# A Fourier mixing layer with a gated feed-forward block: the first batch's stage of one kernel rearranged

## The chip, the cores and the metric

The kernel runs on one core of a Trainium2 chip. The core has a matrix engine (PE, with its weight loads shown as PEld), three engines for elementwise work (DVE, ACT, POOL), a sync engine (SP) that here only issues transfers, and 16 DMA engines that all queues share. Each engine works through its own instructions in the order written and waits on semaphores for the others. The metric is device time in microseconds (us), the median of several runs of the whole kernel.

## The reference

Input `x` is 8 batches of 3008 rows of 256 columns. Each batch gets a two-dimensional discrete Fourier transform, over the rows and over the columns, of which the real part is kept. The 24064 rows that result go through a gated feed-forward block with 1536 hidden columns.

```python
X = np.fft.fft(x, axis=1)
X = np.fft.fft(X, axis=2)
h = X.real                                  # 24064 x 256
g = h @ w_gate
out = (g / (1 + np.exp(-g)) * (h @ w_val)) @ w_out
```

## The kernel before

**The mathematics that the code uses.** The real part of the transform is a sum of cosine products less a sum of sine products. Row k and row 3008-k of a batch share both sums and differ in the sign of the second, so the kernel computes a tile `Pt` (cosine sums) and a tile `Qt` (sine sums) for half of the rows, 1504 per batch. The transform over the 256 columns is put into the weights once: `Wp` is the cosine table `CD` times the weights, `Wq` is the sine table `SDt` times the weights, for the gate and for the value matrix, and `Wm` is `Wq` scaled for the mirrored row.

**Folding.** The rows of a batch are split into four sets (`a` = 0 to 3) of 752. In each set a row that rises with the index is paired with one that falls, and in each pair column d is added to column 256-d, so that the sums run over a quarter of the data. The pairs 1 to 128 of each set form the long set, `XA`, and the last 60 the short set, which for the first batch is `XC0`: four slots of two halves of the partitions. The rises are in slots 0 to 3 of `XA` (0 and 1 of `XC0`), the falls in slots 4 to 7 (2 and 3).

**The first stage** computes the P and Q tiles 0 and 1, for the first batch, before the steady work can start. It is written out by hand, engine by engine (`tc.manual_schedule()`), and its steps are:

- The sync queue issues the loads: all of the long set's rises in one transfer of 1 MB, two falls, the short set's rises and falls. ACT's queue issues two falls (`fall_a`), POOL's queue one short load of middle rows and the weights (`load_w`), which it converts to bf16 on the way.
- PE runs 48 products of zeros (line 306), whose results nobody reads.
- The falls lie in another row order than the rises. A product with a 0/1 matrix (`place`, lines 433 to 442) turns the rises' rows over into the falls' order, in PSUM: `putA` for the long set, `putC` for the short one. These matrices are an iota compared with the partition's number.
- DVE adds rises and falls, the columns reversed (`cross`, or `cross_halves`, which does it in two halves), and adds or subtracts the halves (`half_fold`, line 460); `ends` does column 0. POOL does some of these folds (`fold_d`, line 497) and ACT casts the results to bf16 (`half_cast`).
- The cosine and sine tables `Tab` come from POOL (`turns`, line 364), DVE (`angles`, `magnitude`, lines 368 and 372) and ACT (`sine`, `cosine`).
- PE multiplies the folds with the tables into accumulators in PSUM: `acc[0]` are the even sums (P), `acc[1]` the odd ones (Q), each for the even columns' half q=0 and for q=1. `half_folded` adds the long set, `folded_c` the short set, `row0` some single rows.
- ACT copies `acc[eo][0]` (`even_copy`, line 517), and DVE adds it to and subtracts it from `acc[eo][1]` (`first_puts`, line 646), which gives the columns of `Pt` and `Qt`.
- `first_w` (line 505) multiplies the first 512 columns of the weights by `CD` and `SDt`, for the gate (`first_w(0, ...)`) and for the value matrix (`first_w(1, ...)`); the copies that it returns cast the products into `Wp` and `Wq`.
- `turn_signs` and `row_signs` compute a few signs per partition that later tables need.

**The steady work** goes over 24 tiles of 480 or 512 columns of P and Q and 12 blocks of 128 hidden columns: 288 units. In each PE forms the gate and the value for the rows and for the mirrored rows (`mm`, line 1015), ACT the SiLU, DVE and POOL the products, and one tile later PE multiplies by `w_out` (line 1279). In tile 0 every value product stays in its PSUM buffer, one of three, until DVE has multiplied it twice: `hp` (line 1053) for the rows, `hm` (line 1074) for the mirrored ones. The order of the steady work on every engine is computed when the kernel is built, by a planner with costs, windows and due times; it does not depend on when things happen on the chip. Between the units stand the remaining blocks of the weights (lines 1501 to 1516), and POOL's folds and the transforms of the next batches.

PSUM has eight banks of 512 float32 columns. Before, eight pools of one bank each serve both the first stage and the steady work: three `psG`, three `psV`, two `psO`.

## Time and profile before

| | us |
|---|---|
| median of 3 runs (lowest, highest) | 597.34 (597.27, 597.76) |
| profiled execution | 597.77 |
| its span, from the first to the last instruction | 596.0 |
| PE busy in the span | 590.9 |

The profile is one execution. A row of a timeline gives the start in us from the span's start, the duration, the engine, the line of the kernel, the operation, what it writes and reads with the shapes, and how many instructions the row merges; brackets tell how long the engine stood idle before it and who ended that. The ends of matmuls are modelled and overlap with the next one's start, so the distance between two starts is a better price of a matmul than its duration. DMA rows are packets, megabytes and the share of the time of 16 engines.

### The profile page before, as it was taken

How to read it: one execution, taken by the hardware profiler on the slowest of the kernel's cores; microseconds unless marked ns; L12 is line 12 of the kernel's file. 1: busy time of each engine (PE TensorE's matmuls, PEld its weight loads, DVE VectorE, ACT ScalarE, POOL GpSimd, SP SyncE). 2: the span in 40 equal slices, each digit the busy share in tenths (PEclk: the TensorE clock that was granted, in tenths of full speed). 3: DMA queues.
4: the chain of work that ended last, by engine and by line, in shares of the span. 5: the costliest groups of instructions: out<-in, count | busy, mean ns of one | idle time of the engine just before them, and what ended most of it. 6: DMA issues, size and time to landing. Idle time of an engine off the chain costs nothing.

```text
span 596.0 us, 12394 instructions
## 1 busy us (share of the span) xinstructions
PE 590.9 (99%) x4014; PEld 390.6 (66%) x4014; DVE 568.6 (95%) x1062; ACT 553.6 (93%) x1071; POOL 533.5 (90%) x491
## 2 busy tenths in 40 slices
PE   9999999999999999999999999999999999999997
PEld 6456676666666666666666666666666666666686
DVE  9989999999999999999999999999999999999993
ACT  8768989999998899899999999999999999999995
POOL 9979999999999999999899998999889868687782
PEclk9999999999999999999999999999999999999999
DMA  9976772756244255285125122054121103202212
GB/s 251 161 222 229 185 235 71 194 165 222 82 149 126 73 139 137 68 273 159 54 82 168 37 64 63 19 152 143 46 63 37 47 19 88 67 28 63 60 54 81
DMA packets 61070, 68.17 MB, mean 114 GB/s; under 512 B 6744, under 2 KB 48668, under 8 KB 61006
## 3 DMA queue, kind: packets, MB, share of 16 engines
q1 hardware_dynamic: 57422, 64.44, 36.1%
q0 software_dynamic: 3216, 2.36, 2.9%
q8 instruction: 31, 0.51, 0.4%
q10 hardware_dynamic: 368, 0.59, 0.3%
q14 instruction: 33, 0.27, 0.2%
HBM read 40.21 MB, written 35.43 MB: 127 GB/s over the span
## 4 chain that ended last, share of the span: by engine, by line
PE 96%; DVE 0%; ACT 0%; issue 0%
PE o L1279 41%; PE g L1015 27%; PE v L1015 21%; PE g L1453 2%; PE o L1453 2%; PE v L1279 1%; PE o L1501 1%; PE g L622 0%; PE o L622 0%; PE g L1279 0%; PE o L1582 0%; PE g L1650 0%; DVE Wp L508 0%; ACT es L1289 0%; DVE Qt L646 0%
## 5 line engine op out<-in xcount | busy, mean ns | idle before, releaser
L1226 POOL TENSOR_TENSOR hm<-sv 128x1024 bf16<-128x1024 f32 (+2 forms) x137 | 254.7, 1862 | 32.3 <-ACT sv L1202 12.9
L1218 DVE SCALAR_TENSOR_TENSOR sv<-es,v 128x512 f32<-128x512 f32 (+2 forms) x262 | 174.0, 670 | 5.9 <-PE v L1015 4.3
L1279 PE MATMUL o<-Wo,hm 128*128 128x256 bf16 (+1 forms) x1128 | 163.7, 273 | 0.0
L1279 PE MATMUL o<-Wo,hp 128*128 128x256 bf16 (+1 forms) x1104 | 161.1, 272 | 0.0
L1229 DVE TENSOR_TENSOR hp<-sp,v 128x512 bf16<-128x512 f32 (+2 forms) x228 | 151.6, 671 | 1.9 <-PE v L1015 1.1
L1279 PEld LDWEIGHTS <-hm 128*128 128x128 bf16 (+2 forms) x1140 | 111.9, 98 | 58.0 <-issue 0.6
L1279 PEld LDWEIGHTS <-hp 128*128 128x128 bf16 (+2 forms) x1140 | 111.8, 98 | 55.3 <-issue 0.3
L1202 ACT ACTIVATE sv<-g 128x512 f32<-128x512 f32 (+2 forms) x181 | 119.0, 675 | 3.6 <-PE g L1015 3.1
L1127 ACT ACTIVATE sp<-g 128x512 f32<-128x512 f32 (+2 forms) x181 | 112.1, 621 | 5.9 <-PE g L1015 4.0
L1015 PE MATMUL g<-Pt,Wp 128*128 128x512 bf16 (+2 forms) x288 | 107.5, 374 | 0.0
L1015 PE MATMUL v<-Pt,Wp 128*128 128x512 bf16 (+2 forms) x288 | 106.2, 375 | 0.2 <-DVE Wp L508 0.2
L1015 PE MATMUL g<-Qt,Wq 128*128 128x512 bf16 (+2 forms) x288 | 105.4, 375 | 0.1
L1088 ACT ACTIVATE v<-bc,w 128x512 f32<-128x512 bf16 (+2 forms) x139 | 100.3, 726 | 1.9 <-DVE sv L1218 1.0
L1152 DVE SCALAR_TENSOR_TENSOR es<-bc,w,v 128x512 f32<-128x512 bf16 (+2 forms) x135 | 97.9, 732 | 2.1
L1150 ACT ACTIVATE es<-v 128x512 f32<-128x512 f32 (+2 forms) x139 | 86.0, 621 | 3.2 <-PE v L1015 1.6
L1015 PEld LDWEIGHTS <-Wp 128*128 128x128 bf16 x576 | 56.3, 98 | 26.0 <-DVE Wp L508 1.0
L1015 PE MATMUL g<-Qt,Wm 128*128 128x512 bf16 (+2 forms) x195 | 73.1, 376 | 0.0
L1131 DVE SCALAR_TENSOR_TENSOR sg<-bc,w,g 128x512 f32<-128x512 bf16 (+2 forms) x93 | 67.3, 724 | 1.6 <-PE g L1015 1.4
L1235 POOL TENSOR_TENSOR hp<-sp,pp 128x512 bf16<-128x512 f32 (+1 forms) x46 | 57.2, 1245 | 8.0 <-ACT pp L1232 7.8
L1202 ACT ACTIVATE sv<-sg 128x512 f32<-128x512 f32 (+2 forms) x93 | 63.6, 695 | 0.5 <-DVE sg L1195 0.5
L1195 DVE SCALAR_TENSOR_TENSOR sg<-sg,g 128x512 f32<-128x512 f32 (+2 forms) x93 | 61.6, 663 | 0.2
L1015 PEld LDWEIGHTS <-Wq 128*128 128x128 bf16 x437 | 42.7, 98 | 27.5 <-issue 0.4
(218 smaller groups left out, 788.7 us busy)
## 6 DMA issues: line engine op xcount, KB each, us to landing
out_dram<-ev SPq DMA_DIRECT2D x96, 128.0 KB
XA<-in_x_dram SPq DMA_DIRECT2D x30, 256.0 KB
tA<-in_x_dram SPq DMA_DIRECT2D x28, 256.0 KB
XA<-tA SPq DMA_DIRECT2D x14, 512.0 KB
XC<-in_x_dram SPq DMA_DIRECT2D x28, 120.0 KB
tC<-in_x_dram SPq DMA_DIRECT2D x28, 120.0 KB
XC<-tC SPq DMA_DIRECT2D x6, 480.0 KB
bc<-br SPq DMA_DIRECT2D x19, 128.0 KB
```

The costliest lines, as they stand in the source:

```text
L1015: nc.tensor.matmul(ps[:, :n], Wt[:, gv, fs], src[:, :n], start=start, stop=stop, skip_group_check=True)
L1088: nc.scalar.activation(T_[kv][:, :w], bc[t][:, :w], AF.Copy, scale=w0[:, 1, f:f + 1])
L1127: nc.scalar.activation(sp_to()[:, :w], T_[kg][:, :w], AF.Silu)
L1131: nc.vector.scalar_tensor_tensor(T_[keg][:, :w], bc[t][:, :w], w0[:, 0, f:f + 1], T_[kg][:, :w], op0=Alu.mult, op1=Alu.add)
L1150: nc.scalar.activation(T_[kes][:, :w], T_[kv][:, :w], AF.Copy, scale=2.0 if on_pool(u) > 1 else 1.0)
L1152: nc.vector.scalar_tensor_tensor(T_[kes][:, :w], bc[t][:, :w], w0[:, 1, f:f + 1], T_[kv][:, :w], op0=Alu.mult, op1=Alu.add)
L1195: nc.vector.scalar_tensor_tensor(T_[kgm][:, :w], T_[keg][:, :w], 2.0, T_[kg][:, :w], op0=Alu.mult, op1=Alu.subtract)
L1202: nc.scalar.activation(sv()[:, f % 2, w - 1::-1, 1], T_[kgm if by_dve else kg][:, :w], AF.Silu)
L1218: nc.vector.scalar_tensor_tensor(sv()[:, f % 2, w - 1::-1, 0], T_[kes][:, :w], 2.0, T_[kv][:, :w], op0=Alu.mult, op1=Alu.subtract)
L1226: nc.gpsimd.tensor_tensor(hts_(t)[1][:, f - 1:f + 1, :w], sv()[:, :, :w, 1], sv()[:, :, :w, 0], op=Alu.mult)
L1229: nc.vector.tensor_tensor(hts_(t)[0][:, f, :wp], T_[ksp][:, :wp], T_[kv][:, :wp], op=Alu.mult)
L1279: nc.tensor.matmul(st["ps"][:n, j, :], hts[t][minus][:, f, c:c + n], Wo[:, f, :], start=(f == 0), stop=(f == nF - 1))
```

## The change

It touches the first stage only. The steady work has the same instructions in the same order on every engine.

- The long set's rises are loaded by two transfers, sets 0 and 1 and sets 2 and 3, with the falls between them; one of the falls changes queue.
- The middle rows of the short set are loaded by the sync queue, between its first two falls, and no longer by POOL.
- `putA` is filled and compared on POOL, between the two `turns`, and no longer on DVE.
- There are 33 products of zeros at the start and 6 after the placements, instead of 48 and 8.
- PSUM is laid out by six pools of its own while the first stage runs, two of them of two banks; the pools of the steady work are made after it. Sets 2 and 3 of the long set share a tile of two banks, and so do the two sets of the short set; `cross_halves` (long set), `half_fold` and `ends` take both at once. The short set is still crossed one set at a time.
- On PE both pairs of `first_w` come earlier: those of the gate ahead of the short set's even sums, those of the value matrix ahead of all odd sums. The odd sums and `row0` go first through q=0, then through q=1, and ACT's copy of q=0 stands between.
- On DVE `turn_signs` goes behind all `first_puts`, and the cast of the first value weights ahead of the second ones.
- On POOL the sums `EOb` of the odd half go ahead of the next weights' load, and `row_signs` and a memset go behind the first stage's other work. On ACT `weigh_ce` goes behind the casts, and the clearing of `Z0` behind `opposite(1)`.

```diff
+    first_ctx = ExitStack()
+    banks = [first_ctx.enter_context(tc.tile_pool(name=f"bank{i}", bufs=1, space=bass.MemoryType.PSUM)) for i in range(6)]
+    def two_banks(i):
+        return banks[i].tile([P, 2, T], F32, name=f"b{i}")
+    def one_bank(i):
+        return banks[i].tile([P, T], F32, name=f"b{i}")
...
-    q.dma_start(out=XA3[:, 0:4, :], in_=up_block(0, 1, P))
+    def rises_a(a):
+        q.dma_start(out=XA3[:, a:a + 2, :], in_=rows_at(0, R * a + 1, [[2 * D, P], [R * D, 2], [1, 2 * D]]))
...
+    rises_a(0)
     nc.scalar.activation(w0[:, 0, 0:1], zero, AF.Silu)
     fall_a(3, nc.scalar)
-    fall_a(2, q)
-    fall_a(1, nc.scalar)
+    rises_a(2)
+    fall_a(2, nc.scalar)
+    fall_a(1, q)
     fall_a(0, q)
     rises_c(q)
...
-    for a in range(2):
-        fall_c(1, a, q)
-        fall_c(0, a, q)
+    fall_c(1, 0, q)
+    q.dma_start(out=XC0[NCR:64 + NCR + 1:64, 2:4, 0], in_=rows_at(0, 0, [[2 * R * D, 2], [R * D, 2], [1, D]]))
+    fall_c(0, 0, q)
+    for hi in (1, 0):
+        fall_c(hi, 1, q)
...
+    warm(33)
...
-    vts(putA, putA, scalar1=pcol, scalar2=None, op0=Alu.is_equal)
...
     turns(ti[0], kf, 0)
+    nc.gpsimd.iota(putA, pattern=[[-LA, NA], [1, LA]], base=JA - 1, **iota)
+    pts(putA, putA, scalar1=pcol, scalar2=1.0, op0=Alu.is_equal, op1=Alu.mult)
     turns(ti[1], kf, 1)
     more_iotas()
-    nc.gpsimd.dma_start(out=XC0[NCR:64 + NCR + 1:64, 2:4, 0],
-                        in_=rows_at(0, 0, [[2 * R * D, 2], [R * D, 2], [1, D]]))
...
+    b0, b1, b23, bC = one_bank(1), one_bank(4), two_banks(0), two_banks(5)
+    ps0, ps1, ps23, psC = (of_sets(b) for b in (b0, b1, b23, bC))
+    for a, to in enumerate((b0, b1, b23[:, 0], b23[:, 1])):
+        place(to, XA, putA, a)
+    idle = bC
+    warm(6)
...
-    for a in range(2, 4):
-        cross_halves(FA[:, a, :, 1:P + 1], XA, psA, a)
-    for a in range(2, 4):
-        half_fold(0, EOA[0][1][:, a - 2], FA[:, a, :, 1:P + 1], psA, a)
-    for a in range(2, 4):
-        ends(Eh[:, a], XA, psA, a)
+    cross_halves(FA[:, 2:4, :, 1:P + 1], ps23, down23)
+    half_fold(0, EOA[0][1], FA[:, 2:4, :, 1:P + 1], ps23)
+    ends(Eh[:, 2:4], ps23, down23)
...
-    cross_halves(FC[:, 0], XC0, psC, 0)
-    half_fold(0, EB[:, 0, 0], FC[:, 0], psC, 0)
+    for a in range(2):
+        cross_halves(FC[:, a], psC[:, a], downC[:, a])
+    half_fold(0, EB[:, 0], FC, psC)
+    half_fold(1, EB[:, 1], FC, psC)
+    ends(Ec0, psC, downC)
+    first_ws = two_banks(0)
+    copies = [first_w(0, k, 1, first_ws[:, k]) for k in range(2)]
     folded_c(0, 0)
-    copies = [first_w(0, k, 1, p_.tile([P, T], F32, name=n_)) for k, (p_, n_) in enumerate(((psG, "g"), (psV, "v")))]
-    cross_halves(FC[:, 1], XC0, psC, 1)
-    half_fold(0, EB[:, 0, 1], FC[:, 1], psC, 1)
     folded_c(0, 1)
     od0 = even_copy(0)
+    second_ws = two_banks(5)
+    copies += [first_w(1, k, k, second_ws[:, k]) for k in range(2)]
+    start_acc(1, 1, 4)
...
     first_puts(0, od0, (0, 1))
+    for c in copies:
+        c()
     for i in range(2):
+        half_folded(1, 0, False, (i,))
         row0(0, i, acc[1][i])
-    copies[0]()
-    copies[1]()
-    turn_signs()
-    od1 = even_copy(1)
-    copies += [first_w(1, k, k, psO.tile([P, T], F32, name="o")) for k in range(2)]
-    first_puts(1, od1, (0,))
-    for c in copies[2:4]:
-        c()
-    first_puts(1, od1, (1,))
+        if i == 0:
+            od1 = even_copy(1)
+    first_puts(1, od1, (0, 1))
+    turn_signs()
     tmp_ctx.close()
+    first_ctx.close()
+
+    psG = Slots("psG", 3, space=bass.MemoryType.PSUM)
+    psV = Slots("psV", 3, space=bass.MemoryType.PSUM)
+    psO = Slots("psO", 2, space=bass.MemoryType.PSUM)
```

103 lines of the change are left out of this document (41 added, 62 removed).

## The prediction

> **What bounds the kernel.** I read the page's busy shares and chain first, then the timeline of each engine over the first 36 us.
>
> ```profile
> span 596.0 us, 12394 instructions
> PE 590.9 (99%) x4014; PEld 390.6 (66%) x4014; DVE 568.6 (95%) x1062; ACT 553.6 (93%) x1071; POOL 533.5 (90%) x491
> ...
> PE 96%; DVE 0%; ACT 0%; issue 0%
> ```
>
> PE carries the chain. The timeline of PE (start, duration, engine, line, operation, count, idle time before it in brackets) shows where it is not yet PE that decides:
>
> ```profile
> 1.04 5.30 PE L306 MATMUL o<-sel 128*128 128x128 bf16 x48 [1.04 <-DVE sel L258]
> 6.13 0.94 PE L438 MATMUL g<-XA,putA 128*128 128x512 f32 x1
> 7.33 1.02 PE L438 MATMUL v<-XA,putA 128*128 128x512 f32 x2
> ...
> 10.36 1.08 PE L438 MATMUL o<-XC,putC 128*128 128x512 f32 x2
> ...
> 14.00 0.59 PE L505 MATMUL g<-W,CD 128*128 128x512 bf16 x2
> 14.87 0.32 PE L493 MATMUL v<-Tab,EOf 128*128 128x378 bf16 x1
> ...
> 18.20 0.57 PE L1015 MATMUL g<-Pt,Wp 128*128 128x480 bf16 x2
> 18.90 0.36 PE L1015 MATMUL g<-Qt,Wq 128*128 128x480 bf16 x1
> 19.50 0.38 PE L1015 MATMUL v<-Pt,Wp 128*128 128x480 bf16 x1 [0.24 <-DVE Wp L508]
> ...
> 29.76 0.37 PE L1015 MATMUL v<-Pt,Wp 128*128 128x480 bf16 x1
> ```
>
> The steady work begins at 18.20, pauses until 18.90 for the first Q tile and until 19.50 for the cast of the first value weights; after that PE has no idle time worth a row. The first stage is worth what it moves the products at 18.90 and 19.50, if the engines that feed the next 16 us keep up. DVE runs it nearly without a pause:
>
> ```profile
> 3.50 0.61 DVE L355 TENSOR_SCALAR putA<-putA,pcol 128x128 f32<-128x128 f32 x1
> 4.02 1.36 DVE L368 SCALAR_TENSOR_TENSOR rr<-kf,mM,t 128x377 f32<-128x377 f32 x2
> ...
> 7.84 0.68 DVE L447 TENSOR_TENSOR FA<-g,XA 128x510 f32<-128x510 f32 x1
> ...
> 8.44 0.68 DVE L447 TENSOR_TENSOR FA<-v,XA 128x510 f32<-128x510 f32 x1
> ...
> 9.25 0.43 DVE L451 TENSOR_TENSOR FA<-g,XA 128x256 f32<-128x256 f32 x1
> ...
> 10.91 0.41 DVE L460 TENSOR_TENSOR XA<-FA,g 128x256 f32<-128x256 f32 x1
> ...
> 11.71 0.41 DVE L451 TENSOR_TENSOR FC<-o,XC 128x256 f32<-128x256 f32 x1
> ...
> 12.62 0.42 DVE L460 TENSOR_TENSOR EOf<-FC,o 128x256 bf16<-128x256 f32 x1
> ...
> 15.73 1.20 DVE L646 TENSOR_TENSOR Pt<-g,od 128x188 bf16<-128x188 f32 x5 [0.64 <-ACT od L517]
> ...
> 16.92 0.47 DVE L345 TENSOR_SCALAR n__445<-mm 128x4 int32<-128x4 f32 x1
> ...
> 18.07 0.77 DVE L646 TENSOR_TENSOR Qt<-g,od 128x188 bf16<-128x188 f32 x3
> ...
> 20.17 1.40 DVE L1053 TENSOR_TENSOR hp<-sg,v 128x480 bf16<-128x480 f32 x2 [0.25 <-ACT sg L1050]
> ...
> 28.94 0.64 DVE L1074 TENSOR_TENSOR hm<-sg,v 128x480 bf16<-128x480 f32 x1
> ```
>
> The timelines of POOL and ACT, and the sync queue's issues:
>
> ```profile
> 1.45 0.39 POOL L286 IOTA putA<- 128x128 f32 x1
> 2.13 2.86 POOL L364 TENSOR_SCALAR t<-kf,mM 128x377 int32<-128x377 f32 x4
> 6.45 0.84 POOL L406 TENSOR_SCALAR putC<-putC,pcol 128x128 f32<-128x128 f32 x1
> 8.32 0.82 POOL L394 DMA_DIRECT2D W<-in_moe_w_gate_dram  x1
> 18.89 1.35 POOL L512 TENSOR_SCALAR Wm<-Wq,m 128x512 bf16<-128x512 bf16 x2
> ...
> 15.23 0.47 ACT L517 COPY od<-v 128x377 f32<-128x377 f32 x1 [0.78 <-PE v L493]
> 17.10 0.47 ACT L517 COPY od<-v 128x377 f32<-128x377 f32 x1 [0.42 <-PE v L628]
> ...
> 3.90 3.88 SPq L270 DMA_DIRECT2D XC<-in_x_dram  x4
> ```
>
> And the DMA view (packets, MB, share of the 16 engines): q1, the sync engine's queue, from 0 to 4 us; q1 and q10 (ACT's) from 7.0 to 7.5; q1 and q0 (POOL's) from 11.0 to 11.5; then the value weights' issue with its KB and us to landing.
>
> ```profile
> q1 hardware_dynamic: 266, 0.54, 46.0%
> ...
> q1 hardware_dynamic: 58, 0.10, 53.6%
> q10 hardware_dynamic: 52, 0.09, 48.5%
> ...
> q0 software_dynamic: 69, 0.07, 84.4%
> q1 hardware_dynamic: 32, 0.04, 33.3%
> ...
> W<-in_moe_w_val_dram POOLq DMA_DIRECT2D x1, 256.0 KB, 4.8
> ```
>
> **The change, step by step** (starts in us of the profiled execution).
>
> 1. *The test that makes putA goes from DVE to POOL.* DVE saves 4.02 - 3.50 = 0.52. On POOL the iota (0.39) and the test (0.84 at most, the row of putC) now stand between the two pairs of turns (0.72 each). From about 2.0 POOL runs: two turns to 3.4, putA to 4.65, two turns to 6.1. DVE's run from 4.02 to 7.84 starts at 3.50; its fourth angle operation is due at 6.13 and needs the last turn, so it is covered by hardly anything: 0 here, and 0.1 for each 0.1 that POOL is later. The crossing starts at 7.32.
>
> 2. *Rises in halves, 33 idle products instead of 48.* At 0.110 each (5.30 over 48) PE is free at 4.7, when putA is there. Half of the 1 MB, the first two sets, had left the queue by 4.0 (0.54 MB), so sets 0 and 1 can be placed from 4.7, two by two matmuls of 0.43 (7.33 to 8.19), and are no longer what DVE waits for. Sets 2 and 3 come behind one fall: 0.78 MB more at 0.38 MB/us (the two queues' 0.19 from 7.0 to 7.5), 6.0, and some 0.9 to land, which is the time from the end of the rises' packets (half a megabyte more at q1's full rate, about 5.3) to the placement at 6.13: 6.9, placed by 8.7. The long set's loads move as many bytes as before, so the merged crossing finds the last fall there between 8.73, when DVE is ready, and 9.25, when it was read before; I take 8.85, near the first, for nothing waited at 9.25.
>
> 3. *Sets 2 and 3 two at a time.* Four operations (9.25 to 10.91, 1.66) become two of 512 elements; the nearest row is the 510-element one, 7.84 to 8.44, so 0.60 each. The half fold goes from 0.66 to 0.60, the ends from two to one. DVE is done at 10.75 instead of 11.71: 0.96 earlier.
>
> 4. *The short set.* Here DVE meets the loads. The placement at 10.36 needs the short set's rises. They were there then; PE had no work of the long set left after 9.9, only idle products, so they may have been there up to 0.5 earlier. I take 10.27, near the row; the first pair took 1.08, so DVE can start at 11.35, 0.36 earlier than 11.71 and not 0.96. The first set takes 12.62 - 11.71 = 0.91, to 12.26. The second needs the last fall. Its issue moves back, for a one-row load is now issued among the four (3.88 in all), from 7.8 to about 8.5, and POOL's issue of the gate weights moves forward, from 8.32 to about 7.4 (no load issue of its own and no row signs ahead of it). The last fall's end is not seen in the trace; q1's last packets start before 11.5, and with 0.8 to land it is there at about 12.2. Below: nothing changes, and there is no wait at 12.26. Above: the gate weights go first, whole; at 69 packets in 0.84 of half a microsecond their 256 of 1 KB take 1.6, and the last fall lands near 13.8. I take the value nearest to the rows from 7.0 to 7.5, where two queues shared the engines half and half: the fall, one of four that share 1.6 us of q1, loses its own length, 0.4, and the second set runs from 12.65 to 13.56.
>
> 5. *Two half folds instead of four, and the order on PE.* Even to 14.16, odd to 14.76 (0.60 each), ends to 14.85. The gate weights' products (14.00 to 14.87, 0.87) now stand ahead of the short set's even sums and are done by then. Four products of 0.16 from 14.25; the third ends at 14.89 (0.32 modelled), so ACT's copy starts at 14.93 instead of 15.23, and DVE's first puts run from 15.45 to 16.72. The value weights' products follow on PE, 14.90 to 15.77. They are a new wait ahead of the odd sums: the load is issued at about 9.75 and lands 4.8 later, 14.6; cover 0.3. If it is later, everything behind it on PE is, one for one. Odd sums of the short set (0.65), of the long set (0.32) and the heads (0.4) follow: ACT's second copy at 17.2 instead of 17.10, PE done at 17.95. DVE casts the value weights in the gap (16.72 to 17.32) and starts the second puts at 18.0 instead of 18.07. So the product of 18.90 comes at 18.83, and that of 19.50, whose cast is long done, at 19.03: 0.47 earlier.
>
> 6. *The turn signs go behind the second puts.* Before, they ran in a hole (16.92 to 18.07, 1.15). Now DVE is done with the puts at 19.27 and the signs stand in front of the first hp, which is queued behind them. Three operations of four elements: 0.4 at least (three of the shortest, 0.15), 1.15 at most. I take 0.9, nearer to their own row: POOL is as busy then. The first hp starts at 20.17, just as before.
>
> 7. *Tile 0.* From 20.17 to 29.58 (28.94 + 0.64) DVE has 0.1 us of idle time, and the product at 29.76 takes the PSUM buffer that the hm at 28.94 sets free. PE, 0.47 early, waits there: it keeps 29.76 - 29.58 less a 0.06 signal, 0.12.
>
> 8. *Costed at nothing.* The doubling of the first Wq (18.89) starts near 19.5, behind the row signs and a memset; its reader on PE comes 2.5 later. The next weights' load is issued 1.9 later and still lands before 19.0, with PE at 20.5. Clearing Z0 behind two table operations lets the sync queue go on 0.55 later; POOL's fold of the next batch, which waits for that queue, would start at most 0.55 later, and no row shows PE waiting for it. Without these covers each costs its own shift, 0.5 at most.
>
> **Sum:** -0.12 us. The profiled execution took 597.77 (span 596.0 and 1.8 around it), 0.43 over the median of the runs, 597.34; the sum is taken off the median: **597.2**. A difference under 0.2%, 1.2 us, can hardly be told from none here.
>
> **Rivals.**
>
> *A, the gate weights pass the last fall (slower).* The upper end of step 4: 13.8 instead of 12.65 moves all that follows by 1.15, the first hp too, so no buffer in tile 0 takes any of it back: +1.0, 598.3. It decides from a landing past 12.8. For it: the two issues change places. Against it: q1 still has a backlog when POOL's descriptors arrive.
>
> *B, PE runs its placements slowly (slower).* The first placement's matmul took 0.94, its mates 0.59 (1.02 over two that overlap): PE is slow until about 6.5, after 5.4 us of unbroken products, while the granted clock shows 1.00. Eight matmuls at 0.35 more put set 3 at 11.5 instead of 8.7; the waits of steps 4 (0.6 and 0.4) take back 1.0, and +1.65 is left, +1.5 in the sum: 598.9. It decides if PE runs empty after 4.7, because putA or the first half is late. The Trainium skill's page "TensorE: Matmul & The Clock Gate", section "Part 1: The HAM clock gate (the 'warmup' mystery)", says that the array starts at half rate and speeds up only after a window of some 3.4 us of activity, whose phase is free; the 0.94 agrees. By that rule fewer idle products and a hole among the placements can cost a whole window, which is this rival.
>
> *C, the loads do not hold DVE (faster).* If the short set is in place when DVE comes (10.75), the whole saving arrives: 0.96, and 0.3 from the merged half folds, with the signs short: -1.3, 596.0. It decides if the short set's rises land 0.6 earlier; the unchanged bytes speak against it.
>
> *D, the later order suffers (slower).* Signs at 1.15, the sync queue 0.55 late, the doubling late: DVE starts tile 0 at 20.4 and POOL lags; +0.3 to +1.5, middle 598.1.
>
> *E, all gain is swallowed:* 597.3 to 597.5, the likeliest case's upper side.
>
> **Chances.** Likeliest case with E 0.44 (its own range 596.7 to 597.7), A 0.18, B 0.14, C 0.10, D 0.14. Half of A and a third of D pass 1.2 us, all of B and C do: faster 0.10, within 0.62, slower 0.28. The range from 596.4 to 598.9 leaves out C and the upper half of B.
>
> **What would show it.** Right: the crossing at 7.3, the merged pair near 8.9 at 0.6 each, a hole on DVE before 11.35, the first copy of ACT near 14.9, the product with Qt within 0.2 of 18.83. Wrong: a long hole before the second short set (A), placements 0.85 apart (B), no hole before 11 (C), PE idle between 20 and 60 us (D). The forecast fails most easily at step 4's 0.4 and step 6's 0.9.

## The result, and the profile after

The changed kernel takes 599.96 us (median of 5 runs, 599.69 to 600.35) beside 597.34 (597.27 to 597.79) of the kernel before: ratio 1.0041, 95% interval 1.0027 to 1.0056. It is 2.6 us slower, where 597.2 was forecast and 598.9 was the end of the range. The profiled execution took 600.07.

The lines that answer to those of the prediction follow, with the same columns (start, duration, engine, line of the changed kernel, operation, count, idle time before it and who ended that). PE's timeline after:

```profile
1.04 3.55 PE L317 MATMUL b<-sel 128*128 128x128 bf16 x33 [1.04 <-DVE sel L265]
...
4.78 1.98 PE L444 MATMUL b<-XA,putA 128*128 128x512 f32 x4 [0.19 <-POOL putA L415]
7.07 1.95 PE L444 MATMUL b<-XA,putA 128*128 128x512 f32 x4 [0.31 <-DMA XA<-in_x_dram]
10.32 1.96 PE L444 MATMUL b<-XC,putC 128*128 128x512 f32 x4 [0.96 <-DMA XC<-in_x_dram]
...
15.04 0.82 PE L491 MATMUL b<-Tab,EOf 128*128 128x377 bf16 x4 [0.61 <-DVE EOf L461]
15.71 0.60 PE L503 MATMUL b<-W,CD 128*128 128x512 bf16 x2
...
19.97 0.36 PE L1020 MATMUL g<-Qt,Wq 128*128 128x480 bf16 x1 [0.47 <-DVE Qt L648]
```

The placements start early, as forecast, and everything from the short set on is late: the first Q product stands at 19.97, before at 18.90. DVE's timeline shows where it happens:

```profile
7.64 0.68 DVE L447 TENSOR_TENSOR FA<-b,XA 128x510 f32<-128x510 f32 x1
...
9.07 0.69 DVE L451 TENSOR_TENSOR FA<-b,XA 128x512 f32<-128x512 f32 x1
9.79 0.70 DVE L452 TENSOR_TENSOR b<-b,XA 128x512 f32<-128x512 f32 x1
10.53 0.69 DVE L461 TENSOR_TENSOR XA<-FA,b 128x512 f32<-128x512 f32 x1
11.13 0.15 DVE L456 TENSOR_TENSOR Eh<-b,XA 128x4 f32<-128x4 f32 x1
12.31 0.42 DVE L451 TENSOR_TENSOR FC<-b,XC 128x256 f32<-128x256 f32 x1 [1.03 <-PE b L444]
...
13.37 0.42 DVE L451 TENSOR_TENSOR FC<-b,XC 128x256 f32<-128x256 f32 x1 [0.16 <-DMA XC<-in_x_dram]
...
19.13 1.20 DVE L648 TENSOR_TENSOR Qt<-b,od 128x188 bf16<-128x188 f32 x5 [1.03 <-ACT od L515]
...
20.31 0.56 DVE L358 TENSOR_SCALAR n__428<-mm 128x4 int32<-128x4 f32 x1
20.91 0.63 DVE L359 TENSOR_SCALAR n__428<-n__428 128x4 int32<-128x4 int32 x1
21.57 0.36 DVE L360 TENSOR_SCALAR turn_sign<-n__428 128x4 f32<-128x4 int32 x1
22.77 1.22 DVE L1058 TENSOR_TENSOR hp<-sg,v 128x480 bf16<-128x480 f32 x2 [0.84 <-ACT sg L1055]
```

DVE leaves the long set at 11.2 (before 11.71) and then stands for 1.03 until PE has placed both halves of the short set. The signs take 1.62 us (20.31 to 21.93), and the first `hp` starts at 22.77 instead of 20.17. ACT's timeline says why that is later still than the end of the signs:

```profile
14.14 0.82 ACT L546 ACTIVATE Z<-zero 128x768 bf16<-128x768 f32 x1
15.73 0.47 ACT L515 COPY od<-b 128x377 f32<-128x377 f32 x1 [0.77 <-PE b L491]
...
18.13 0.59 ACT L506 CAST Wq<-b 128x512 bf16<-128x512 f32 x1 [0.95 <-DVE Wp L506]
18.61 0.48 ACT L515 COPY od<-b 128x377 f32<-128x377 f32 x1
22.17 1.03 ACT L1055 ACTIVATE sg<-g 128x480 f32<-128x480 f32 x2 [3.08 <-POOL XA L376]
```

The first SiLU (the last row) idles 3.08 and starts only when the signs are done, though its input, the product at 19.97, was there by about 20.3. The engine named as its releaser is POOL; the runs below show that DVE's signs, which end 0.24 before it, were the ones. Z0 is cleared at 14.14. The timelines of the sync queue and of POOL after show what else moved:

```profile
5.04 0.62 SPq L304 DMA_DIRECT2D XC<-in_x_dram  x1
6.96 2.69 SPq L279 DMA_DIRECT2D XC<-in_x_dram  x3
14.99 0.77 SPq L548 DMA_DIRECT2D XC<-Z  x1
...
3.62 1.10 POOL L415 TENSOR_SCALAR putA<-putA,pcol 128x128 f32<-128x128 f32 x1
...
14.48 0.74 POOL L406 DMA_DIRECT2D XA<-in_moe_w_gate_dram  x1
...
20.13 1.35 POOL L510 TENSOR_SCALAR Wm<-Wq,m 128x512 bf16<-128x512 bf16 x2
21.47 1.60 POOL L376 TENSOR_SCALAR XA<-EOf,mM 128x188 int32<-128x188 f32 x4
...
41.01 2.35 POOL L188 TENSOR_TENSOR SDf<-XC 128x1020 f32<-128x1020 f32 x1 [2.11 <-DMA XC<-tC]
```

The rows of the same instructions in the timelines of the kernel before, and its first SiLU:

```profile
13.74 0.77 SPq L548 DMA_DIRECT2D XC<-Z  x1
...
12.03 0.73 POOL L394 DMA_DIRECT2D XA<-in_moe_w_gate_dram  x1
...
39.17 2.35 POOL L181 TENSOR_TENSOR SDf<-XC 128x1020 f32<-128x1020 f32 x1 [1.95 <-DVE hp L1053]
...
19.43 0.57 ACT L1050 ACTIVATE sg<-g 128x480 f32<-128x480 f32 x1 [0.44 <-PE g L1015]
```

The clearing of the unused rows, from which the sync queue goes on to the next batch's loads, is issued 1.25 later; POOL's first fold of that batch starts 1.84 later; the next block's gate weights are issued 2.45 later.

To follow a lateness through the kernel, the start of each ACT instruction is set against the same instruction of the kernel before (both from one profiled execution). This table holds it in us at four places (by the time in the kernel before), beside the time. The label is that of the run below; the medians and ratios are against runs of the kernel before on the same chip, taken together with it.

| kernel | at 30 | at 70 | at 130 | at 590 | median (before) | ratio, 95% |
|---|---|---|---|---|---|---|
| changed | 1.68 | 1.68 | 2.04 | 2.46 | 599.96 (597.34) | 1.0041 (1.0027 to 1.0056) |
| e1 signs early | 0.70 | 1.23 | 1.67 | 1.50 | 599.90 (597.74) | 1.0032 (1.0021 to 1.0042) |
| e2 signs in own room | 0.75 | 1.23 | 1.67 | 1.52 | 599.57 (597.74) | 1.0026 (1.0016 to 1.0035) |
| e3 odd copy first | 1.89 | 1.89 | 2.25 | 3.04 | 600.09 (597.74) | 1.0037 (1.0024 to 1.0049) |
| e4 before, signs late | 0.46 | 0.47 | 0.48 | 0.64 | 598.43 (597.74) | 1.0011 (1.0002 to 1.0020) |
| e5 Z0 first | 1.57 | 1.57 | 1.93 | 1.73 | 599.77 (597.55) | 1.0038 (1.0025 to 1.0052) |
| e6 signs early, Z0 first | 0.56 | 0.55 | 0.91 | 0.64 | 598.62 (597.55) | 1.0021 (1.0013 to 1.0030) |
| e7 before, Z0 late | -0.45 | 1.40 | 1.46 | 1.35 | 598.88 (597.55) | 1.0015 (1.0005 to 1.0025) |
| e8 e6, short set apart | 0.90 | 0.89 | 0.90 | 0.68 | 598.54 (597.55) | 1.0015 (1.0006 to 1.0024) |
| e9 e8, other orders | 0.98 | 0.99 | 1.01 | 1.25 | 598.94 (597.75) | 1.0019 (1.0009 to 1.0028) |
| e10 e9, middle rows on POOL | 1.08 | 1.10 | 1.12 | 1.55 | 599.25 (597.75) | 1.0023 (1.0014 to 1.0032) |
| e11 e8, weights' loads early | 0.12 | 0.12 | 0.13 | 0.38 | 597.99 (597.74) | 1.0001 (0.9992 to 1.0010) |
| e12 before, signs in first hole | -0.45 | 1.15 | 1.26 | 1.35 | 597.68 (597.74) | 0.9997 (0.9988 to 1.0007) |
| e13 e12, Z0 earlier | -0.36 | -0.35 | -0.34 | -0.39 | 597.52 (597.78) | 0.9993 (0.9984 to 1.0002) |
| e14 e12, Z0 at 10 us | -0.48 | -0.49 | -0.46 | -0.53 | 598.14 (597.78) | 1.0003 (0.9994 to 1.0012) |
| e15 e11, Z0 at 10 us | 1.87 | 1.88 | 1.87 | 1.83 | 599.66 (597.78) | 1.0029 (1.0017 to 1.0042) |
| e16 before, loads late | 1.16 | 1.18 | 1.15 | 1.07 | 598.44 (597.54) | 1.0016 (1.0008 to 1.0025) |
| e17 before, three late | 1.01 | 2.94 | 3.01 | 3.09 | 598.94 (597.54) | 1.0027 (1.0016 to 1.0037) |

A row is one execution and can lie above or below its median: those of e12 and e17 are the slowest of their kernels' executions, those of e5, e6, e13 and e14 the fastest.

### The profile page after: what moved, and what is told of

The parts are those of the page before. It is cut to its first block, busy times and chain, and to the rows that moved or that the text cites. A ratio compares the mean times of both kernels' runs of the same rounds, so it can differ in the third digit from the quotient of the medians.

```text
span 598.3 us, 12296 instructions
## 1 busy us (share of the span) xinstructions
PE 586.9 (98%) x3937; PEld 388.5 (65%) x3997; DVE 568.2 (95%) x1054; ACT 553.8 (93%) x1071; POOL 533.9 (89%) x491
## 4 chain that ended last, share of the span: by engine, by line
PE 91%; DVE 2%; issue 1%; ACT 1%; DMA 1%; SPq 0%; ACTq 0%; DVEq 0%
PE o L1284 40%; PE g L1020 25%; PE v L1020 20%; PE g L1458 2%; PE o L1458 2%; PE v L1284 1%; DMA out_dram<-ev 1%; PE o L1506 0%; PE o L624 0%; PE g L624 0%; DVE es L1157 0%; DVE sg L1136 0%; DVE sv L1223 0%; PE g L1284 0%; DVE sg L1200 0%
## 5 line engine op out<-in xcount | busy, mean ns | idle before, releaser
L1020 PE MATMUL g<-Pt,Wp 128*128 128x512 bf16 (+2 forms) x278 | 103.7, 374 | 0.4
L1020 PE MATMUL g<-Qt,Wq 128*128 128x512 bf16 (+2 forms) x251 | 92.7, 374 | 1.1 <-DVE Qt L648 0.5
L1020 PE MATMUL g<-Qt,Wm 128*128 128x512 bf16 (+2 forms) x189 | 70.8, 375 | 0.8 <-ACT sg L1055 0.6
```

Of the source, the lines that this page charges most:

```text
L1020: nc.tensor.matmul(ps[:, :n], Wt[:, gv, fs], src[:, :n], start=start, stop=stop, skip_group_check=True)
```

## The experiments

### The signs and the first SiLU: e1, e2, e4

e1 puts the signs back in front of the second puts:

```diff
     for c in copies:
         c()
+    turn_signs()
...
     first_puts(1, od1, (0, 1))
-    turn_signs()
```

> Edit: in the changed kernel the three turn sign operations go back in front of the second puts, into DVE's hole between the cast of the value weights (ends 18.10) and the second puts (19.13). Theory 1 (the first SiLU waits for the signs, since it writes into space that the first stage gives up only when its last user there, the signs, is done): the first SiLU starts about 20.5 instead of 22.17, right behind its products; the first hp near 21.4 instead of 22.77; the whole kernel gains what separates its lateness in tile 0 (1.68) from that of the first Q product (19.97 against 18.90 before, 1.07), 0.6 us, and more if the 0.8 that is lost after 110 us follows from it: 598.6 to 599.4. Rival (the lateness of the odd sums alone sets the end, the signs are hidden by three value buffers): within 0.2 of the changed kernel. Rival (the signs cost only their DVE time in front of the first hp, as the prediction had it): the SiLU stays at 22.17 or follows the hp, not the signs.

e2 leaves them where they are, but lets them use no tile of the first stage (`mM` holds the same numbers divided by M and is kept for the whole run):

```diff
-        n_ = col("n_", 4, I32)
-        vts(n_, mm_, scalar1=0.5, scalar2=0.25, op0=Alu.mult, op1=Alu.add)
+        n_ = turn_sign.bitcast(I32)
+        vts(n_, mM, scalar1=0.5 * M, scalar2=0.25, op0=Alu.mult, op1=Alu.add)
```

> Edit: the changed kernel with the signs where they are, but their intermediate is kept in the result's own storage and they read a table that is kept for the whole run, so that they use no space that the steady work takes over. DVE does the same three operations at the same place. Theory 1 (the wait is for space): the first SiLU starts near 20.5, though the signs still end near 21.9; the first hp follows the signs, near 22.0 instead of 22.77; a gain of about half of that of the kernel with the signs early, 0.3 to 0.8. Rival (SiLU waits for the sign values or for DVE's time as such): SiLU stays at 22.17 and the time is that of the changed kernel within 0.2.

e4 does the change's move in the kernel before:

```diff
-    turn_signs()
     od1 = even_copy(1)
...
     first_puts(1, od1, (1,))
+    turn_signs()
```

> Edit: the kernel before with the turn signs behind the second puts and nothing else changed. Theory 1: the second puts start where they did (they waited for the odd copy) and end near 19.9; the signs run to about 21.2 and the first SiLU, 19.43 before, waits for them: it starts near 21.3, the first hp near 21.9 instead of 20.17; 1.0 to 1.6 us slower than before, 598.3 to 598.9. Rival (the prediction's view, the signs stand in front of the first hp and cost DVE time alone, and the kernel before had 1.15 of hole that goes): 0 to 0.5 slower. Rival (the lateness in the changed kernel comes from its odd sums): the kernel before keeps 597.3.

ACT's and DVE's timelines of e2:

```profile
20.37 1.05 ACT L1055 ACTIVATE sg<-g 128x480 f32<-128x480 f32 x2 [1.40 <-DMA XC<-in_x_dram]
...
20.19 0.68 DVE L358 TENSOR_SCALAR turn_sign<-mM 128x4 int32<-128x4 f32 x1
...
21.85 1.21 DVE L1058 TENSOR_TENSOR hp<-sg,v 128x480 bf16<-128x480 f32 x2
```

With the signs in the same place and as long, the first SiLU starts at 20.37, right behind its product, and no longer waits for them. So it was not the value of the signs nor DVE's time: the SiLU writes into space that the first stage gives up (`tmp_ctx.close()`), and waits for the last operation that uses it. Whether it would wait for any user of that space or only for one at its own place, e2 does not tell. With the signs early (e1) it starts at 20.33. In the kernel before the late signs do the same, as ACT's timeline of e4 shows:

```profile
20.95 1.03 ACT L1050 ACTIVATE sg<-g 128x480 f32<-128x480 f32 x2 [1.99 <-DMA XC<-Z]
```

The signs end at 20.71 in e4, again 0.24 before the SiLU. Without them it stood at 19.43, and e4 is 0.7 slower by its median, less than the 1.0 that was expected, since the second puts also start earlier (17.58 instead of 18.07). Yet against their own runs of the kernel before e1 is still 2.2 slower and e2 1.8, where the changed kernel is 2.6 (e1's 599.90 lies above the 598.6 to 599.4 that was expected): their lateness of 0.7 at 30 grows again by 70 and by 130. That was the next question.

### The sync queue's chain: e5, e6, e7

e5 clears Z0 first, as before; e6 is e1 and e5 together.

```diff
+    nc.scalar.activation(Z0.rearrange("p q k d -> p (q k d)"), zero.to_broadcast([P, 6 * P]), AF.Copy)
     weigh_ce()
     opposite(1)
-    nc.scalar.activation(Z0.rearrange("p q k d -> p (q k d)"), zero.to_broadcast([P, 6 * P]), AF.Copy)
```

> Edit: in the changed kernel ACT clears Z0 ahead of weigh_ce and opposite(1), as the kernel before has it; nothing else. Theory 2 (besides the late first SiLU there is a second loss beside it: the sync queue's clear_c waits for Z0, 14.99 instead of 13.74, and the loads of the next batch behind it, POOL's first fold of that batch, its products and so PE near 60 and 120 us come late): clear_c at about 13.3, POOL's fold that starts 39.17 before back to within 0.4 of that (41.01 in the changed kernel). The two losses lie side by side, so the lateness of 1.68 in tile 0 stays and the end gains only what comes on top of it later (0.35 near 120 us, 0.5 near 260 us): 599.0 to 599.7. Rival (the sync queue's lateness costs nothing, the later losses follow from tile 0): 599.8 to 600.1.

> Edit: the signs back in front of the second puts and Z0 ahead of weigh_ce and opposite(1). Theory 2 (two losses side by side): where the signs alone left 0.7 in tile 0 that grew to 1.28 at 60 us and 1.5 at the end, the 0.7 now stays: 597.9 to 598.5, about 0.5 to 1.0 above the kernel before and over 1 us under each single edit. Rival (one loss, the first stage's late odd sums): no better than the signs early alone, 599.1 to 599.9.

e7 puts the same line behind `opposite(1)` in the kernel before:

```diff
-    nc.scalar.activation(Z0.rearrange("p q k d -> p (q k d)"), zero.to_broadcast([P, 6 * P]), AF.Copy)
     opposite(1)
+    nc.scalar.activation(Z0.rearrange("p q k d -> p (q k d)"), zero.to_broadcast([P, 6 * P]), AF.Copy)
```

> Edit: the kernel before with the clearing of Z0 behind opposite(1), one operation of ACT later, and nothing else. The first odd and even copies do not depend on it. Theory 2: clear_c 0.75 to 0.85 later (13.74 to about 14.5), POOL's fold of the next batch 0.8 later (39.17 to about 40), and PE, which is not late in tile 0 here, waits for POOL's products near 60 us: 0.3 to 1.0 slower than before, 597.8 to 598.7. The prediction's view (step 8: nothing waits for it, POOL's fold is at most 0.55 later and no row shows PE waiting): within 0.2 of before.

The timelines of the sync queue, POOL, ACT and PE in e7 show the chain:

```profile
14.31 0.76 SPq L548 DMA_DIRECT2D XC<-Z  x1
...
40.91 2.35 POOL L181 TENSOR_TENSOR SDf<-XC 128x1020 f32<-128x1020 f32 x1 [4.15 <-DMA tA<-in_x_dram]
...
60.47 0.65 ACT L1202 ACTIVATE sv<-g 128x512 f32<-128x512 f32 x1 [1.75 <-POOL hm L1226]
...
61.73 0.38 PE L1015 MATMUL v<-Pt,Wp 128*128 128x512 bf16 x1 [1.70 <-ACT v L1088]
```

One operation of ACT, put later in the order, delays the clearing, that the next batch's loads, those POOL's fold, the fold POOL's products, these ACT's buffer, and 47 us later PE stands still for 1.70. The clearing comes 0.57 later here and the fold 1.74. e7's median is 1.3 above before, more than the 0.3 to 1.0 expected. It is not lost in every execution: 9 of e7's 11 took 598.0 or more, and so did 5 of the 27 of the kernel before beside them, so the later clearing makes common what was rare. In the changed kernel the loss does not show by itself: PE is 1.68 late already, and the two lie side by side. By the medians over their own runs of the kernel before, undoing one alone gives 0.4 to 0.8 of the 2.6 (e1, e5, e2), hardly more than the intervals tell; undoing both (e6) gives 1.5. Both e5 (599.77) and e6 (598.62) ended 0.1 above what was expected of them.

### The short set and ACT's order: e3, e8, e10

e3 lets ACT copy the odd sums ahead of its cast of the second value weights, for which that copy stood at 18.61.

```diff
-    for c in copies:
+    for c in copies[:3]:
         c()
...
             od1 = even_copy(1)
+            copies[3]()
```

> Edit: in the changed kernel ACT copies the odd sums ahead of its cast of the second value weights; that cast waited for DVE's cast of the first ones (18.13), with the copy queued behind it. Theory: the copy starts near 18.0 instead of 18.61, the second puts near 18.5 instead of 19.13, the first Q product near 19.4 instead of 19.97; the signs then end near 21.3, SiLU and all behind it come 0.5 to 0.6 earlier: 599.3 to 599.5. Rival (two wide PSUM tiles make no wait of their own and the copy waits for the odd sums on PE): no shift, 599.8 to 600.1.

It missed. The copy came to 18.30, but the second puts then waited 0.99 for PE's last odd sums and started at 19.22: what is late is PE's odd sums. The cast's wait cost nothing.

e8, on top of e6, gives each half of the short set a bank of its own and folds it as soon as it is crossed; the two products of the value weights get a bank each too.

```diff
-    for a in range(2):
-        cross_halves(FC[:, a], psC[:, a], downC[:, a])
-    half_fold(0, EB[:, 0], FC, psC)
-    half_fold(1, EB[:, 1], FC, psC)
-    ends(Ec0, psC, downC)
+    for a in range(2):
+        cross_halves(FC[:, a], psC[a], downC[:, a])
+        for eo in range(2):
+            vtt(EB[:, eo, a], FC[:, a][:, :, ::-1], psC[a][:, :, P:D], op=SUMS[eo])
+    for a in range(2):
+        ends(Ec0[:, a], psC[a], downC[:, a])
```

> Edit: on top of the signs early and Z0 first, the two sets of the short set are placed into a bank of their own each, and each is folded as soon as it is crossed (four half folds instead of two); the value weights' two products have a bank each too. Theory 3 (a tile of two banks is handed over as one: DVE waited 1.03 at 12.31 until both sets were placed): the first short crossing starts near 11.4 instead of 12.31, the second stays near 13.2 behind the last fall, the last even fold ends near 14.5 instead of 14.9, ACT's first copy near 15.2, the first Q product near 19.3, 0.3 to 0.6 earlier than with both edits alone: 597.4 to 598.1. Rival (DVE waited for the second placement's data all the same, or the last fall alone sets the time): the first crossing stays after 12.0, or the copies do not move, and the time is that of the two edits.

DVE's timeline of e8:

```profile
11.38 0.42 DVE L451 TENSOR_TENSOR FC<-b,XC 128x256 f32<-128x256 f32 x1
```

DVE starts on the short set at 11.38, the 11.35 of the prediction, where e6 waited until 12.23: the wait at 12.31 was for the whole two-bank tile. But the gain stops there. The last even sums waited 0.40 for ACT's `opposite(1)`, and the first Q product came 0.2 earlier than in e6 (19.55 against 19.75); the times of e6 and e8 do not differ, and e8's 598.54 misses the 597.4 to 598.1 expected.

e10 moves the middle rows back to POOL's queue and folds the even halves first, on top of e9 (below):

```diff
-    q.dma_start(out=XC0[NCR:64 + NCR + 1:64, 2:4, 0], in_=rows_at(0, 0, [[2 * R * D, 2], [R * D, 2], [1, D]]))
...
     more_iotas()
+    nc.gpsimd.dma_start(out=XC0[NCR:64 + NCR + 1:64, 2:4, 0], in_=rows_at(0, 0, [[2 * R * D, 2], [R * D, 2], [1, D]]))
```

> Edit: on top of the previous one, the load of the middle rows goes back to POOL's queue (ahead of the test that makes putC), and of the four half folds the even ones come first. It tells what made the last fall late (13.2 instead of 12.2): theory 3b, the sync queue's one issue more, for it holds the last three falls until 6.96 and issues the last at about 9.65; without it they are out by about 8.7 and the second short crossing starts at once behind the first set's fold, near 12.7; ACT's first copy near 14.8. Rival A (the gate weights share the engines with the last fall): they are now issued 0.8 later, near 8.6, and the fall lands early for that reason as well, which the time of issue alone cannot part, but if the fall stays near 13.2 with its issue at 8.7, sharing is the cause. Time 597.0 to 598.0, 0 to 0.4 under the previous kernel; more than 0.4 later if the gate weights now come after PE is ready for them (13.3).

The falls were issued until 8.54 instead of 9.65, but the first crossing now waited 0.80 for a load (until 12.01), the second came at 13.27 without a wait, and the time, 599.25, was no better (597.0 to 598.0 was expected). It does not part the later issue from the sharing with the gate weights; what the last fall costs is in any case small (idle 0.16 in the changed kernel).

### The next block's weights: e9, e11, e16

e9, on top of e8, puts `weigh_ce` back ahead of `opposite(0)`, and the row signs and the memset ahead of POOL's last fold.

```diff
+    weigh_ce()
     opposite(0)
...
-    weigh_ce()
     opposite(1)
...
+    row_signs()
+    nc.gpsimd.memset(sel[0:1, :], 1.0)
     fold_d(1, 2)
...
-    row_signs()
-    nc.gpsimd.memset(sel[0:1, :], 1.0)
```

> Edit: the kernel with the signs early, Z0 first and the short set apart, and besides weigh_ce back ahead of opposite(0) on ACT (so that opposite(1), for which the last even sums waited 0.40 at 15.02, ends near 14.0) and POOL's row signs and memset moved in front of its last fold of the first batch (so that the doubling of the first Wq, 20.13 in the changed kernel and 18.89 before, comes 0.6 earlier). Theory 4 (what is left over the kernel before is made of ACT's and POOL's late orders): the last even sums near 14.5, ACT's first copy near 15.0, the first Q product near 19.2, PE near 0.3 late in tile 0 instead of 0.9: 597.3 to 598.1. Rival (the odd sums' new place behind the value weights' products, which land and end late, is what holds the first Q product): the first Q product stays after 19.4 and the time within 0.3 of the kernel with three edits.

The first Q product did not come earlier (19.73, the rival's side), the time of 598.94 lies above the range, and a new wait appeared, here in PE's timeline of e9:

```profile
25.56 0.61 PE L1507 MATMUL o<-XA,CD 128*128 128x512 bf16 x2 [0.50 <-DMA XA<-in_moe_w_gate_dram]
```

POOL had issued those weights still later (the first at 15.12). e11 keeps e9 except for POOL: its order is that of the kernel before, with the short set's heads ahead of the second issue and the row signs last.

```diff
-    fold_d(1, 2)
-    ptt(EOb[:, 1, 0:2], EOA[1][0], EOA[1][1], op=Alu.add)
     load_w(1, (0,))
+    fold_d(1, 2)
...
     heads(hd[:, 0], hd[:, 1], CEa)
+    ptt(EOb[:, 1, 0:2], EOA[1][0], EOA[1][1], op=Alu.add)
...
-    load_w(1, (1,))
     heads(Ec0[:, 0], Ec0[:, 1], CEc)
+    load_w(1, (1,))
```

> Edit: signs early, Z0 first, weigh_ce back ahead of opposite(0), the short set apart (one set at a time, a bank each), and POOL's order as in the kernel before (the next block's gate weights are issued ahead of the last fold of the first batch, the sums for the odd half behind the heads), with the short set's heads ahead of the next issue; row signs and memset stay where the change put them. Theory 5 (the next weights' loads are the third chain beside the signs and Z0: with the two others undone PE waited 0.50 at 25.56 for the gate weights' landing): that wait is gone, the first Q product comes near 19.3, PE is about 0.3 late in tile 0 and stays so: 597.3 to 598.2. Rival (the wait at 25.56 follows from what else shares the DMA engines, not from the issue): it stays, and the time is that of the kernel with five edits, 598.5 to 599.2.

The wait is gone, PE is 0.12 late from tile 0 to 130 us, and the time is that of the kernel before (ratio 1.0001). e16 puts POOL's order of the change into the kernel before (the gate weights behind the odd half's sums):

```diff
-    load_w(1, (0,))
     fold_d(1, 2)
+    ptt(EOb[:, 1, 0:2], EOA[1][0], EOA[1][1], op=Alu.add)
+    load_w(1, (0,))
...
     heads(hd[:, 0], hd[:, 1], CEa)
-    ptt(EOb[:, 1, 0:2], EOA[1][0], EOA[1][1], op=Alu.add)
```

> Edit: the kernel before with POOL's order of the change for the next block's gate weights: they are issued behind the last fold of the first batch and the sums of the odd half, 2.4 later (12.03 to about 14.4). Theory 5: the landing that PE waited 0.50 for at 25.56 in the kernel with five edits undone (issued at 15.12) becomes late here too: PE waits 0.2 to 0.8 near 24.5 and the kernel is 0.1 to 0.7 slower. The prediction's view (step 8: it still lands with time to spare): within 0.2.

PE's timeline of e16, at the products that before started at 24.48:

```profile
25.74 0.60 PE L1501 MATMUL o<-XA,CD 128*128 128x512 bf16 x2 [0.72 <-DMA XA<-in_moe_w_gate_dram]
```

0.9 slower by the median, above the 0.1 to 0.7 expected. The block's gate weights were issued 2.7 later (14.76 for 12.03), but PE waits for those of the block after it, issued only 0.5 later (17.13 for 16.67). They land later, most likely because the first block's load, which used to be out of the way by then, now shares the queue with them; no run parts this from the other queues' traffic. The DMA view from 8 to 27 us has both gate loads in one row (KB of one, median us from issue to landing); the kernel before and e16:

```profile
XA<-in_moe_w_gate_dram POOLq DMA_DIRECT2D x2, 256.0 KB, 5.5
```

```profile
XA<-in_moe_w_gate_dram POOLq DMA_DIRECT2D x2, 256.0 KB, 7.3
```

In the changed kernel no such wait shows: PE comes to these products later than the weights do.

### Three orders in the kernel before: e17

e17 has the edits of e4, e7 and e16 at once, with all tiles, banks, folds and PE's order as before.

> Edit: the kernel before with three of the change's orders and nothing else: the signs behind the second puts, Z0 behind opposite(1), the next gate weights behind the odd half's sums. If these orders are the loss, they lie partly side by side: about 0.5 in tile 0 from the signs, the same or a little more with the loads, and near 60 us the sync queue's chain on top: 1.2 to 2.0 over the kernel before, 598.9 to 599.7. If the shared banks and the new order on PE are what matters, no more than 1.0 over it.

1.4 us by the medians, over half of the change's 2.6. The three alone cost 0.7, 1.3 and 0.9, 2.9 in all: half of it lies side by side.

### Can the gain in tile 0 be had? e12, e13, e14, e15

e12 puts the signs of the kernel before into DVE's hole ahead of the first puts:

```diff
+    turn_signs()
     first_puts(0, od0, (0, 1))
...
-    turn_signs()
     od1 = even_copy(1)
```

> Edit: the kernel before, with the turn signs in DVE's hole ahead of the first puts (0.64, in which it waits for ACT's first copy) in place of the hole ahead of the second ones. If the signs themselves held the second puts (18.07, while ACT's second copy was done at 17.57), the second puts start near 17.6, the first Q product near 18.6 and the first value product near 19.0: PE 0.45 earlier in tile 0. What follows tells whether the sync queue's chain is already as late as PE bears in the kernel before: if it is not, the end is 0.3 to 0.45 earlier, 597.1 to 597.4 beside a kernel before of 597.6; if it is, PE waits near 60 us and the time is that of before within 0.15.

The second puts came to 17.60 and the first Q product to 18.60, as expected. In the profiled execution, the slowest of 11, POOL's fold started at 40.66 although the clearing was issued at 13.60, no later than before, and PE lost 1.6 near 60 us. So the loads do not land a fixed time after the clearing, and the kernel before has little to spare there. e13 therefore clears Z0 between ACT's first cast and its copies:

```diff
     half_cast(0, 0)
+    nc.scalar.activation(Z0.rearrange("p q k d -> p (q k d)"), zero.to_broadcast([P, 6 * P]), AF.Copy)
```

e14 clears it still earlier, in the place of `weigh_ce`, and e15 is e11 with Z0 there:

```diff
-    weigh_ce()
+    nc.scalar.activation(Z0.rearrange("p q k d -> p (q k d)"), zero.to_broadcast([P, 6 * P]), AF.Copy)
     opposite(0)
...
-    nc.scalar.activation(Z0.rearrange("p q k d -> p (q k d)"), zero.to_broadcast([P, 6 * P]), AF.Copy)
+    weigh_ce()
```

> Edit: the kernel before with the signs in DVE's first hole and Z0 cleared ahead of ACT's copies of the odd halves instead of behind the casts. Theory 2: Z0 is done near 12.0 instead of 13.7, clear_c and the loads behind it 1.5 earlier, POOL's fold at 38.3 or earlier, no PE wait near 60 us in any run; ACT's copies come 0.2 later and the first puts with them, so tile 0 is 0.2 to 0.4 ahead of before and stays so: 597.1 to 597.4 beside a kernel before of 597.6. Rival (the loads of the next batch land when they do for other traffic's sake): POOL's fold stays after 39 and runs spread from 597.3 to 599 as before.

> Edit: the same, but Z0 is cleared ahead of opposite(0), in the place of weigh_ce, which goes behind the casts. Theory 2: Z0 is done near 10.0, the sync queue's chain starts 3.5 earlier; the loads of the next batch now share the engines with the first batch's last falls and weights (the gate weights landed at 13 before), so the gate weights' products may wait up to 0.5: tile 0 from 0.45 ahead to 0.1 late, and no loss near 60 us: 597.0 to 597.7. Rival: as above.

> Edit: the changed kernel with the signs early, the short set apart, POOL's order as before and Z0 cleared ahead of opposite(0) (weigh_ce stays where the change put it, behind the casts). Beside the kernel without the early Z0, 0.12 late in tile 0 and 0.25 over the kernel before by its median: theory 2 gives the same tile 0 within 0.3 and a smaller spread, median 597.5 to 598.0; rival: no change in the spread.

POOL's fold in the timelines of e12 and e13:

```profile
40.66 2.35 POOL L181 TENSOR_TENSOR SDf<-XC 128x1020 f32<-128x1020 f32 x1 [3.87 <-DVE Qt L1470]
...
37.38 2.35 POOL L181 TENSOR_TENSOR SDf<-XC 128x1020 f32<-128x1020 f32 x1 [0.52 <-DMA tA<-in_x_dram]
```

In e13 it starts at 37.38 and the 0.36 of tile 0 reaches the end. Ten of its 11 executions lie between 597.36 and 597.61, while of the 22 beside it of the kernel before six took 598.65 or more. By the median it is 0.26 ahead of the kernel before, which its interval (0.9984 to 1.0002) does not tell from no change. It is the best of the kernels here, and no proof of a better one. In e14 the jump near 60 us was absent from the profiled execution, the fastest, too, but its executions spread from 597.22 to 598.60; why is not known. e15, expected at 597.5 to 598.0, lost 1.9 at once, on PE:

```profile
16.98 0.59 PE L504 MATMUL b<-W,CD 128*128 128x512 bf16 x2 [1.77 <-DMA W<-in_moe_w_val_dram]
```

With the sync queue's loads 3.8 us earlier than in e11 (the clearing at 9.66 for 13.46) the value weights landed 6.8 us after their issue (4.5 in e11), and in the change's order on PE all odd sums stand behind their products: the wait of which step 5 said that its cover was 0.3.

## Why the prediction was wrong

The front of the stage gained where its steps said, about half as much, and nothing of it reaches the end (e11 keeps it, has its first Q product at 19.27, behind the 18.90 of before, and only equals that kernel); what was forecast as free is what cost.

- **Step 1** (putA on POOL): the crossing came at 7.64, not 7.32. The test on POOL took 1.10 (0.84 was taken as the most), and the turns behind it are what DVE waits for, as the step said.
- **Step 2**: placements from 4.78 (forecast 4.7), the second pair done at 9.02 (8.7), the merged crossing at 9.07 (8.85). Right within 0.3. (Two of the falls change places between the queues, not one.) Rival B fell in this execution: four matmuls in 1.98 from 4.78 on, no slower than the four at 7.07. There is luck in it. The first two matmuls start 0.53 apart here, but 0.95 and 1.02 in the profiled executions of e3 and e15, which begin alike; they still had the second pair done near 9.2, for it waits for its load anyway. The Trainium skill's page "TensorE: Matmul & The Clock Gate" (Part 1) asks for some 3.4 us of activity in a window that does not start with the kernel. The rows agree: the idle products ran from 1.04, 3.7 us before the first placement, and that is enough in one execution and not in another.
- **Step 3** was mis-sized: the two merged crossings took 0.72 and 0.74 to the next start, not 0.60 each (the half fold did take 0.60). DVE was done at 11.2, 0.5 earlier instead of 0.96.
- **Step 4** failed on a wait that it did not list: one tile for both sets makes DVE wait for both placements (12.31 against 11.35). e8 shows the cause. The second set started at 13.37 instead of 12.65. The landing of the last fall was mis-sized as well: about 13.2, where 12.2 was worked out and rival A put its limit at 12.8. The wait for both placements hid all but 0.16 of that. With the tiles apart and the order kept, DVE would have been ready at 12.29 (11.38 and the forecast's 0.91) and have stood for the fall until about 13.2, an estimate that no run shows; so either of the two is enough for nearly the whole delay. Whether the fall was late for rival A's reason, the gate weights, or for its later issue (until 9.65, forecast 8.5) e10 does not part. The sync queue stood still from 5.66 to 6.96, which was not foreseen: its next issue waited there for a load of the long set to land. Why it had to is not shown.
- **Step 5** followed from it: ACT's copies at 15.73 and 18.61 (14.93 and 17.2), the first Q product at 19.97 (18.83). Of the 1.4 by which the second copy is late, some 0.5 is the queue behind ACT's cast, which e3 shows to cost nothing. The wait for the value weights, its named risk, did not come in the changed kernel.
- **Step 6** failed in kind. The signs' own time was sized at 0.9 and took 1.62, and it was counted as DVE time in front of the first `hp`. In fact ACT's first SiLU waits for them, so that SiLU and `hp` follow the signs in turn.
- **Step 7** was not put to the test: PE came to tile 0 late, not early.
- **Step 8** failed in two of the three things that it costed at nothing, and by what the same orders do in the kernel before it has the larger part of the loss. The clearing of Z0 came 1.25 later, not 0.55, and "no row shows PE waiting for it" was true of a profile in which it was just in time: e7 shows 1.3 us. The next weights' load came 2.45 later, not 1.9, and landed 4.3 us after its issue, before 19.0 as the step said; but the step followed that one load alone, and what PE waits for in e16, 0.9 us, is the second load behind it in POOL's queue. For the doubling no wait shows; POOL's small operations were not moved alone.

**Rival D** had the two right suspects, signs and sync queue, and priced them at 0.3 to 1.5 where 2.6 was lost; it had the doubling, for which no wait shows, in place of the loads. The three costs were each judged against a kernel in which nothing else is late, and no row of that kernel shows a margin that is merely not yet used up.

**What stays open.** The three orders in the kernel before give 1.4 of 2.6 us; undoing them together with the shared bank and the place of `weigh_ce` (e11) gives back all that can be told. How the other 1.2 divides between the later odd sums, the shared bank and `weigh_ce` was not parted, as the losses cover each other. The step of 0.35 between 110 and 130 us (in the changed kernel, e1, e2, e3, e5, e6) has no shown cause; it is absent wherever the short set lies apart (e8 to e11, e15) and from the kernels made from the one before. The 0.5 near 260 us in the changed kernel ends at an ACT copy that waits 0.44 for an output to be stored, and no run takes that up.

## What to carry to other kernels

An operation that leaves the critical path for the end of a stage can become the last user of the space that the next stage takes over, and then the next stage waits for it, however small it is. An operation or a transfer moved later "under cover" is to be priced by following its queue to the next thing that waits, batches ahead; where such chains lie side by side, undoing one alone shows little, so undo them together and do each alone in the kernel before. A tile over two banks was handed over as one here (e8): merging two operations also merges their waits.

## What was not expected of the hardware

Three operations of four elements took 0.56, 0.63 and 0.36 us on DVE while POOL streamed beside them (20.13 to 23.07), and in e1, where POOL was issuing a transfer, far less, as DVE's timeline of e1 has it:

```profile
17.85 0.16 DVE L358 TENSOR_SCALAR n__408<-mm 128x4 int32<-128x4 f32 x1
18.05 0.17 DVE L359 TENSOR_SCALAR n__408<-n__408 128x4 int32<-128x4 int32 x1
18.25 0.29 DVE L360 TENSOR_SCALAR turn_sign<-n__408 128x4 f32<-128x4 int32 x1
```

In the changed kernel POOL's two doublings (1.35 in all from 20.13) end near 20.82 and 21.48 and its next operation near 21.88; the signs end at 20.87, 21.54 and 21.93, each 0.05 to 0.06 behind one of them. The Trainium skill's page "SBUF — State Buffer", section "Who interferes with whom", says that a DVE `tensor_scalar` can run in a mode that needs the port pair shared with GpSimd, and that whichever of the two issues first then has the pair for its whole instruction while the other is blocked. The rows agree.

A chain of loads ended over 1 us later although its start was issued no later: POOL's fold stands at 39.17 in the kernel before and at 40.66 in e12, with the clearing at 13.74 and 13.60. And with the sync queue's loads 3.8 us earlier a load of 256 KB on POOL's queue took 6.8 us from issue to landing, 4.5 without that (e15 and e11).
